# Order of products in the attention pieces, and later slots for three planned steps, in a fused attention and feed-forward kernel

## The chip, the cores and the metric

The kernel runs on one core of a Trainium2 chip. The metric is the device time of one execution in microseconds (us), taken as the median of several runs; less is better. One execution was also recorded by the hardware profiler, and all rows shown come from that record. TensorE is called PE there (its weight loads PEld), VectorE is DVE, ScalarE is ACT, GpSimd is POOL, and SyncE, which issues nearly all DMAs here, is SP.

## What is computed

A decayed linear attention, cut into blocks, feeds a feed-forward network in which two linear maps are multiplied with each other. Batch 4, 8 heads, sequence 768, head size 64; 3072 tokens, model width 512, inner width 1536.

```python
for b in range(nb):                       # blocks of the sequence
    intra = einsum('bhic,bhjc->bhij', qb, kb) * Dmask      # scores, masked
    intra = einsum('bhij,bhjd->bhid', intra, vb)
    inter = einsum('bhid,bhde->bhie', qb * lam_pow, kv_state)
    out[:, :, sl] = intra + inter
    kv_state = lam_block * kv_state + einsum('bhsd,bhse->bhde', kb_dec, vb)
x = out.transpose(0, 2, 1, 3).reshape(B * S, H * D)
return ((x @ w_a) * (x @ w_b)) @ w_out
```

## The kernel before

**Units and groups.** The kernel takes blocks of 128 positions, so a batch has six, and there are 24 units of work (unit u is block u % 6 of batch u // 6; units 5, 11, 17 and 23 are the last blocks of their batches). Units are gathered in groups of 4, 1, 2, 4, 4, 4, 4 and 1 (line 28). The feed-forward part works on one group at a time while the attention of later units is done in between.

**The feed-forward part** (`ffn`, line 518) of a group has slots. In slots 0 to 11, slot f computes inner columns f: four matmuls into an `a_ps` bank, four into a `b_ps` bank (line 468), a copy of the first to SBUF on ScalarE (line 477), and their product `ab` on VectorE (line 495). After them come two slots for each unit of the group, each with half of the output matmuls (`op`, line 515). After each slot `hook` issues the attention steps that `PLAN` (line 43) has for it. Group 2 holds units 5 and 6 and so has slots 0 to 15; group 3 holds units 7 to 10 and has slots 0 to 19.

**The steps in PLAN.** Each engine does its instructions in the order in which they are issued; the schedule is manual, so the order of the program is the order of each queue.
- `P u` prepares a unit. `prep_k` (line 298, alone `PK`) scales k and q on GpSimd (line 276; on VectorE for the k of a few early units), and for units from 7 on issues the DMA transpose of both on SP (line 304). `prep_v` (line 309, alone `PV`) casts v to bf16 on VectorE (line 295; on GpSimd for early units) and calls `pump` (line 188), which issues on SP the loads of q, k and v (line 130) that are next in order, as far ahead as `LOOKAHEAD` and `used["u"]` allow.
- `S u` computes a unit's scores, k by q, into two PSUM banks (`scores`, line 326: 8 matmuls with a 64-row contraction, alternating between the two row halves of the array), and masks them on VectorE (line 349).
- `V u` adds the unit to the running state in PSUM (line 396) and copies it to SBUF on VectorE (`st`, line 429). For the last block of a batch it does nothing.
- `Q (a, b, c, d)` is the pair piece, `pieces_O` (line 442). It takes four banks for the scores of c and d and two for the outputs of a and b, then issues on TensorE: `inter` of a and b (line 380: 8 matmuls a unit, 64 by 64, so that four tiles of the array are in use; none for the first block of a batch; the state of the unit before is read), `scores` of c and d, `intra` of a and b (line 382, masked scores by v), with ScalarE's copies of the outputs to the next groups' x (line 389). Then follow the state products of b for units from 9 on (line 418 or 396), the masks of c and d, and the copy of b's state. `O2` and `O` are the same without c and d.

**Buffers that set order.** PSUM has seven banks in a rotation (`ps_bank`, line 110): `a_ps`, `b_ps`, `op`, scores and outputs all take the next one, and a feed-forward tile skips the bank of the feed-forward tile just before it. `qkT`, the transposed q and k, has five buffers, the loaded q, k and v four each, v in bf16 and scaled q and k six each, the state `st` four. A wait is set for whoever last read a buffer.

Of the kernel before, what the change touches and what calls it, by code (L numbers as in the profile page):

```python
# [22 lines left out]
def _bc(ap, dims):  # L23
# [23 lines left out]
    1: [(0, "V", 4), (2, "T", 5), (3, "PK", 6), (6, "PV", 6), (6, "S", 5), (7, "T", 6),  # L47
        (10, "S", 6), (12, "O2", (5, 6)), (13, "P", 7)],
    2: [(0, "V", 6), (1, "P", 8), (4, "P", 9), (7, "V", 7),
        (9, "S", 7), (9, "S", 8), (6, "P", 10), (10, "V", 8),  # L50
        (12, "Q", (7, 8, 9, 10)), (12, "P", 11), (13, "V", 9), (14, "P", 12),
        (14, "O2", (9, 10))],
    3: [(4, "S", 11), (4, "S", 12)],
}
for _g, _u in ((3, 11), (4, 15), (5, 19)):
    PLAN.setdefault(_g, []).extend(
        [(1, "P", _u + 2), (3, "P", _u + 3), (4, "V", _u),
         (7, "Q", (_u, _u + 1, _u + 2, _u + 3)), (10, "P", _u + 4),
         (12, "P", _u + 5), (13, "V", _u + 2), (16, "Q", (_u + 2, _u + 3, _u + 4, _u + 5))])
PLAN[3] += [(_s, "W", None) for _s in range(12, 19)]  # L60
PLAN[5] = [(_s, _n, (21, 22, 23) if _us == (21, 22, 23, 24) else _us)
# [5 lines left out]
def kernel(  # L67
# [12 lines left out]
    B, H, S, D = q.shape  # L80
# [29 lines left out]
    def ps_bank(name, shape, dt, hold=False, ffn=False, at=None):  # L110
        i = bank["next"] if at is None else at
        while i in bank["held"] or (ffn and i == bank["ffn"]):
            i = (i + 1) % 7
        if ffn:
            bank["ffn"] = i
        bank["next"] = (i + 1) % 7
        if hold:
            bank["held"].add(i)
        return ps_pool.tile(shape, dt, name=name, tag=f"ps{i}")
# [203 lines left out]
    def score_banks():  # L323
        return [ps_bank(f"kq{i}", [128, HP, 128], F32) for i in range(2)]

    def scores(u, kq=None):
        d = U[u]
        kq = kq or score_banks()
        for hp in range(HP):
            for i in range(2):  # L330
                p = slice(64 * i, 64 * i + 64)
                nc.tensor.matmul(kq[i][:, hp, :], lhsT=d["kT"][p, hp, :], rhs=d["qT"][p, hp, :],  # L332
                                 start=True, stop=True, skip_group_check=True)
        return kq

    def masks(u, kq):
        ms = mask(kq)
        U[u]["m"] = lambda i, hp: ms[i][:, hp, :]
# [14 lines left out]
    def o_banks(us, ats=(None, None)):  # L353
        for b, at in enumerate(ats):
            ps = ps_bank("o_ps", [128, 2, 2, BLK], F32, at=at)
            for n, u in enumerate(us):
                U[u].setdefault("o", []).append(ps[:, :, n, :])
        for u in us:
            U[u]["new"] = {(b, half): u == us[0] for b in range(2) for half in range(2)}
            U[u]["flags"] = U[us[0]]["new"]  # L360
# [9 lines left out]
    def inter(u):  # L370
        if u % NB > 0:
            st = st_bufs[(u - 1) % 4]
            for c in range(HP):
                for b in range(2):
                    p = slice(64 * b, 64 * b + 64)
                    o_mm(u, b, c, lhsT=st[p, c, b, :], rhs=U[u]["qT"][p, c, :])

    def intra(u, b):
        for c in range(HP):
            o_mm(u, b, c, lhsT=U[u]["vb"][:, 4 * b + c, :], rhs=U[u]["m"](b, c))  # L380

    def evac_o(us, b, eng="act"):
        xT, col = xTs[us[0]]
        n = len(us)
        o = U[us[0]]["o"][b]
        src = _bc(o, [o.ap[0], [2 * BLK, 2], [1, n * BLK]])
        dst = xT[:, 2 * b:2 * b + 2, col:col + n * BLK]
        if eng == "act":
            nc.scalar.copy(dst, src)  # L389
        else:  # L390
            nc.vector.tensor_copy(dst, src)
# [19 lines left out]
    def kv_beside(u):  # L411
        if u % NB == 0 or u % NB == NB - 1:
            kv_update(u)
            return
        for c in range(HP):
            for b in range(2):
                p = slice(64 * b, 64 * b + 64)
                nc.tensor.matmul(kv["ps"][p, c, b, :], lhsT=U[u]["kn"][:, 2 * c + b, :],
                                 rhs=U[u]["vb"][:, 4 * b + c, :],
                                 start=False, stop=True, skip_group_check=True)  # L420

    def kv_copy(u, ps, eng="dve"):
        st = st_bufs[u % 4]
        if eng == "act":
            for b in range(2):
                p = slice(64 * b, 64 * b + 64)
                nc.scalar.copy(st[p, :, b, :], ps[p, :, b, :])
        else:
            nc.vector.tensor_mul(st[:].rearrange("p c b d -> p c (b d)"),  # L429
                                 ps[:].rearrange("p c b d -> p c (b d)"), bdiag_bc)  # L430
# [11 lines left out]
    def pieces_O(us, nxt=()):  # L442
        kqs = [score_banks() for u in nxt]
        o_banks(us)
        for u in us:
            inter(u)
        for u, kq in zip(nxt, kqs):
            scores(u, kq)
        for b in range(2):
            for u in us:  # L450
                intra(u, b)
            evac_o(us, b)
        beside = len(us) == 2 and us[0] >= n0 + 5
        if beside:
            kv_beside(us[1])
        for u, kq in zip(nxt, kqs):
            masks(u, kq)
        if beside and us[1] % NB < NB - 1:
            kv_copy(us[1], kv["ps"])
# [245 lines left out]
    for g, n in enumerate(GROUPS):  # L705
# [6 lines left out]
        def hook(slot, plan=plan):  # L712
            for name, us in plan.get(slot, ()):
                if name == "C":
                    cast_w("o", us, "dve")
                elif name == "PK":
                    prep_k(us)
                elif name == "PV":
                    prep_v(us)
                elif name == "P":  # L720
                    prep_k(us)
                    prep_v(us)
                elif name == "W":
                    store_kept()
                elif name == "T":
                    piece_T(us)
                elif name == "S":
                    piece_S(us)
                elif name == "V":
                    piece_V(us)  # L730
                elif name == "O":
                    pieces_O((us,))
                elif name == "O2":
                    pieces_O(us)
                else:
                    pieces_O(us[:2], us[2:])
# [31 lines left out]
```

## Time and profile before

| | |
|---|---|
| median of 6 runs | 233.45 us (233.06 to 233.86) |
| profiled execution | 233.54 us |
| its span, first to last instruction | 231.8 us |
| granted TensorE clock, mean | 0.999 |
| TensorE busy | 224.1 us, 97% of the span |
| VectorE, ScalarE, GpSimd busy | 117.3, 89.1, 51.0 us |
| group 2 to the start of group 3 (62 to 82 us) | TensorE busy 19.9 of 20 us |
| group 3 (82 to 116 us) | TensorE busy 32.8 of 34 us |
| groups 4 and most of 5 (116 to 186 us) | TensorE busy 70.0 of 70 us |
| DMA | 39.4 MB in 97541 packets, mean 170 GB/s |

Times in rows are counted from the start of the span. In a timeline row stand start, length, engine, line, operation, output<-inputs, form and count, and in brackets the engine's idle time before it with what ended it; neighbouring like instructions are merged into one row. The ends of matmuls are modelled, and those of a stream overlap, so the starts are what tells the pace. A chain of waits goes back from the last instruction to what released each step. A wait for several semaphores is put down to the one that came last, which need not be the one that was waited for.

### The profile page before, as it was taken

How to read it: one execution, taken by the hardware profiler on the slowest of the kernel's cores; microseconds unless marked ns; L12 is line 12 of the kernel's file. 1: busy time of each engine (PE TensorE's matmuls, PEld its weight loads, DVE VectorE, ACT ScalarE, POOL GpSimd, SP SyncE). 2: the span in 40 equal slices, each digit the busy share in tenths (PEclk: the TensorE clock that was granted, in tenths of full speed). 3: DMA queues.
4: the chain of work that ended last, by engine and by line, in shares of the span. 5: the costliest groups of instructions: out<-in, count | busy, mean ns of one | idle time of the engine just before them, and what ended most of it. 6: DMA issues, size and time to landing. Idle time of an engine off the chain costs nothing.

```text
span 231.8 us, 4653 instructions
## 1 busy us (share of the span) xinstructions
PE 224.1 (97%) x1839; PEld 121.5 (52%) x1839; DVE 117.3 (51%) x205; ACT 89.1 (38%) x172; POOL 51.0 (22%) x65
## 2 busy tenths in 40 slices
PE   7799999999999999899999999999999999999994
PEld 2475444459687644354544454544454544444493
DVE  1894856636579645864335583335583313331050
ACT  3587464067342342232233332334332334432261
POOL 6060000238451356333301534001200000000000
PEclk9999999999999999999999999999999999999999
DMA  4999999999998999999859996239200220000211
GB/s 144 306 264 352 363 387 277 299 201 221 205 208 174 216 188 235 232 195 231 303 193 205 197 216 103 93 101 207 56 3 0 93 90 0 4 0 23 112 48 45
DMA packets 97541, 39.36 MB, mean 170 GB/s; under 512 B 85488, under 2 KB 92016, under 8 KB 97520
## 3 DMA queue, kind: packets, MB, share of 16 engines
q1 hardware_dynamic: 97232, 39.00, 73.6%
q8 instruction: 14, 0.23, 0.4%
q10 hardware_dynamic: 288, 0.07, 0.1%
q14 instruction: 7, 0.06, 0.1%
HBM read 28.32 MB, written 6.29 MB: 149 GB/s over the span
## 4 chain that ended last, share of the span: by engine, by line
PE 78%; DMA 12%; SPq 5%; POOL 2%; DVE 1%; issue 0%; ACT 0%; POOLq 0%
PE op L515 25%; PE b_ps L468 24%; PE a_ps L468 23%; DMA kf<-in_k_dram 4%; SPq L130 3%; DMA wst<-in_moe_w_b_dram 3%; PE o_ps L366 3%; DMA qkT<-qk 2%; DMA q<-in_q_dram 2%; POOL qk L276 2%; PE kq L332 2%; PE kvd L396 1%; SPq L304 1%; SPq L159 1%; PE tps L318 1%
## 5 line engine op out<-in xcount | busy, mean ns | idle before, releaser
L495 DVE TENSOR_TENSOR ab<-a_sb,b_ps 128x512 bf16<-128x512 bf16 (+2 forms) x96 | 52.1, 552 | 73.6 <-PE b_ps L468 54.7
L468 PE MATMUL b_ps<-xT,wb_sb 128*128 128x512 bf16 (+2 forms) x384 | 76.9, 326 | 0.2 <-DVE wb_sb L175 0.2
L468 PE MATMUL a_ps<-xT,wa_sb 128*128 128x512 bf16 (+2 forms) x392 | 76.9, 323 | 0.0
L477 ACT CAST a_sb<-a_ps 128x512 bf16<-128x512 f32 (+2 forms) x96 | 45.2, 481 | 60.8 <-PE a_ps L468 58.8
L515 PE MATMUL op<-wo_sb,ab 128*128 128x512 bf16 (+2 forms) x312 | 65.6, 363 | 0.0
L468 PEld LDWEIGHTS <-wb_sb 128*128 128x128 bf16 x384 | 34.4, 98 | 29.1 <-DVE wb_sb L175 0.7
L468 PEld LDWEIGHTS <-wa_sb 128*128 128x128 bf16 x392 | 34.6, 98 | 27.6 <-DVE wa_sb L175 0.4
L515 PEld LDWEIGHTS <-ab 128*128 128x128 bf16 x312 | 28.7, 98 | 29.9
L349 DVE TENSOR_TENSOR m<-kq,lotri 128x512 bf16<-128x512 f32 x47 | 29.4, 684 | 17.1 <-PE kq L332 17.1
L276 POOL TENSOR_TENSOR qk<-kf,lp_k 128x512 bf16<-128x512 f32 x18 | 18.8, 1043 | 74.0 <-DMA kf<-in_k_dram 57.0
L276 POOL TENSOR_TENSOR qk<-qf,lp_q 128x512 bf16<-128x512 f32 x20 | 23.1, 1153 | 23.4 <-DMA qf<-in_q_dram 23.4
L510 ACT COPY o_sb<-op 128x512 f32<-128x512 f32 (+2 forms) x19 | 10.3, 541 | 34.0 <-PE op L515 34.0
L389 ACT CAST xT<-o_ps 128x512 bf16<-128x512 f32 (+1 forms) x24 | 12.1, 555 | 19.2 <-PE o_ps L366 19.2
L429 DVE TENSOR_TENSOR st<-kvd,bdiag 128x512 bf16<-128x512 f32 x18 | 12.3, 683 | 3.8 <-PE kvd L396 3.8
L295 DVE CAST vb<-vf 128x512 bf16<-128x512 f32 x17 | 10.4, 614 | 4.3 <-DMA vf<-in_v_dram 4.3
L208 PE MATMUL idle<-idle_sb 128*128 128x512 bf16 (+2 forms) x23 | 7.3, 452 | 1.3 <-DVE idle_sb L203 1.3
L366 PE MATMUL o_ps<-m,vb 128*64 128x128 bf16 x192 | 8.0, 222 | 0.0
L332 PE MATMUL kq<-qkT 64*128 64x128 bf16 x160 | 6.8, 218 | 1.2 <-DMA qkT<-qk 1.2
L295 POOL CAST vb<-vf 128x512 bf16<-128x512 f32 x7 | 4.3, 620 | 13.8 <-DMA vf<-in_v_dram 13.8
L169 ACT CAST wb_sb<-wst 128x1024 bf16<-128x1024 f32 x5 | 5.2, 1047 | 5.1 <-DMA wst<-in_moe_w_b_dram 5.1
L320 ACT COPY qkT<-tps 128x1024 bf16<-128x1024 bf16 x3 | 3.0, 1013 | 9.9 <-PE tps L318 9.9
L366 PEld LDWEIGHTS <-vb 128*64 128x64 bf16 x192 | 5.8, 109 | 1.4
(58 smaller groups left out, 81.2 us busy)
## 6 DMA issues: line engine op xcount, KB each, us to landing
vf<-in_v_dram SPq DMA_DIRECT2D x24, 256.0 KB, 4.7
qf<-in_q_dram SPq DMA_DIRECT2D x20, 256.0 KB, 3.9
kf<-in_k_dram SPq DMA_DIRECT2D x20, 256.0 KB, 4.4
out_dram<-o_sb SPq DMA_DIRECT2D x16, 256.0 KB, 2.0
wst<-in_moe_w_a_dram SPq DMA_DIRECT2D x6, 512.0 KB, 9.0
wst<-in_moe_w_b_dram SPq DMA_DIRECT2D x6, 512.0 KB, 9.3
wst<-in_moe_w_out_dram SPq DMA_DIRECT2D x6, 512.0 KB, 10.8
out_dram<-o_kept SPq DMA_DIRECT2D x7, 256.0 KB, 2.5
```

Source lines behind the costliest of these rows:

```text
L276: eng_of(eng).tensor_mul(dst.rearrange("p (c b) d -> p b c d", b=2), x[:].rearrange("p (b c) d -> p b c d", b=2), lp.rearrange("p (b c) o ...
L295: eng_of(eng).tensor_copy(vb, vf)
L332: nc.tensor.matmul(kq[i][:, hp, :], lhsT=d["kT"][p, hp, :], rhs=d["qT"][p, hp, :], start=True, stop=True, skip_group_check=True)
L349: nc.vector.tensor_mul(m, kq[i], lotri_bc)
L366: nc.tensor.matmul(U[u]["o"][b][p, c // 2, :], start=new[b, h % 2], stop=True, skip_group_check=True, **ops)
L389: nc.scalar.copy(dst, src)
L429: nc.vector.tensor_mul(st[:].rearrange("p c b d -> p c (b d)"), ps[:].rearrange("p c b d -> p c (b d)"), bdiag_bc)
L468: nc.tensor.matmul(ps[:, lo:hi], lhsT=w_sb[:, s, f * 128:(f + 1) * 128], rhs=xT[:, s, lo:hi], start=(s == 0), stop=(s == KS - 1), skip_gro ...
L477: nc.scalar.copy(a_sb[:, :gt], ps[:, :gt])
L495: nc.vector.tensor_mul(ab[:, f, :gt], a_sb[:, :gt], ps[:, :gt])
L510: nc.scalar.copy(o_sb[:, lo:hi], op[:, lo:hi])
L515: nc.tensor.matmul(op[:, lo:hi], lhsT=ab[:, f, t * 128:(t + 1) * 128], rhs=wo_sb[:, f, lo:hi], start=(f == 0), stop=(f == FC - 1))
```

## The change

Three edits. In group 2, `P` of unit 10 in slot 6 is split: `PK` stays, and `PV`, the cast of its v with the pump call, goes to slot 11. In group 3, `S` of units 11 and 12 go from slot 4 to slot 6, the `V` of unit 11 from slot 4 to 6, and the pair piece of units 11, 12, 13 and 14 from slot 7 to 9; groups 4 and 5 keep their slots. In `pieces_O` the scores are issued ahead of the inter products instead of behind them, in all seven pair pieces.

```diff
@@ PLAN @@
     2: [(0, "V", 6), (1, "P", 8), (4, "P", 9), (7, "V", 7),
-        (9, "S", 7), (9, "S", 8), (6, "P", 10), (10, "V", 8),
+        (9, "S", 7), (9, "S", 8), (6, "PK", 10), (10, "V", 8), (11, "PV", 10),
         (12, "Q", (7, 8, 9, 10)), (12, "P", 11), (13, "V", 9), (14, "P", 12),
         (14, "O2", (9, 10))],
-    3: [(4, "S", 11), (4, "S", 12)],
+    3: [(6, "S", 11), (6, "S", 12)],
 }
 for _g, _u in ((3, 11), (4, 15), (5, 19)):
     PLAN.setdefault(_g, []).extend(
-        [(1, "P", _u + 2), (3, "P", _u + 3), (4, "V", _u),
-         (7, "Q", (_u, _u + 1, _u + 2, _u + 3)), (10, "P", _u + 4),
+        [(1, "P", _u + 2), (3, "P", _u + 3), (6 if _g == 3 else 4, "V", _u),
+         (9 if _g == 3 else 7, "Q", (_u, _u + 1, _u + 2, _u + 3)), (10, "P", _u + 4),
          (12, "P", _u + 5), (13, "V", _u + 2), (16, "Q", (_u + 2, _u + 3, _u + 4, _u + 5))])
@@ pieces_O @@
         kqs = [score_banks() for u in nxt]
         o_banks(us)
+        for u, kq in zip(nxt, kqs):
+            scores(u, kq)
         for u in us:
             inter(u)
-        for u, kq in zip(nxt, kqs):
-            scores(u, kq)
```

## Prediction

> **What bounds the kernel now.** I read the page first, then TensorE's waits, then the timeline at each place where TensorE stands still, then the chain of waits back from there.
>
> ```profile
> PE 224.1 (97%) x1839; PEld 121.5 (52%) x1839; DVE 117.3 (51%) x205; ACT 89.1 (38%) x172; POOL 51.0 (22%) x65
> ```
>
> TensorE (PE) is busy 97% of 231.8 us, so only its idle time can be won. Its waits over the whole span (us in total, times, longest) have one row that is not start-up:
>
> ```profile
> PE kq L332 <- DMA qkT<-qk: 1.2, 1, 1.2
> ```
>
> The other five rows, 3.1 us together, lie before 22 us. I then went through the starts of single matmuls after 40 us: N=512 follow each other by 0.216 us, N=128 by 0.053 to 0.056 us; every change of array tiling (128x128, 64x64, 64x128, 128x64) adds 0.092 to 0.102 us. Beyond these there are two stalls. The first, in the pair piece of group 3's slot 7:
>
> ```profile
> 96.90 0.31 PE L366 MATMUL o_ps<-qkT,st 64*64 64x128 bf16 x8
> 97.14 0.40 PE L332 MATMUL kq<-qkT 64*128 64x128 bf16 x8
> 98.74 0.40 PE L332 MATMUL kq<-qkT 64*128 64x128 bf16 x8 [1.21 <-DMA qkT<-qk]
> ```
>
> Columns: start, length, what, idle before and who ended it. Unit 13's last scores start at 97.32; unit 14's should follow 0.05 later and come at 98.74: **1.37 us** lost, because the DMA transpose of unit 14 lands at 98.70. The second, in the pair piece of group 2's slot 12, against the same sixteen inter products elsewhere (133.19):
>
> ```profile
> 75.24 0.74 PE L366 MATMUL o_ps<-qkT,st 64*64 64x128 bf16 x16
> ```
> ```profile
> 133.19 0.42 PE L366 MATMUL o_ps<-qkT,st 64*64 64x128 bf16 x16
> ```
>
> 0.74 against 0.42: the first inter product starts at 75.24, the second (b=1, other o_ps bank) at 75.57 instead of 75.29. That bank was f=11's b_ps; VectorE's product that reads it ends at 75.52 (row 75.11 below). **0.28 us** lost. Why unit 14 is late, from the chain of waits:
>
> ```profile
> 81.61 2.24 POOL qk L276 x2
> 83.86 1.75 SPq L304
> 85.66 0.57 SPq L130
> 86.29 4.14 DMA kf<-in_k_dram
> 90.65 2.32 POOL qk L276 x2
> 92.99 5.70 DMA qkT<-qk
> 98.74 0.40 PE kq L332 x8
> ```
>
> A loop of load, two scalings on GpSimd (POOL), transpose, next load. TensorE is not in it, so moving TensorE's work doesn't move it.
>
> **Group 3's pieces, two slots later.** A slot (a_ps and b_ps, 8 x 0.216) is 1.73 us. The pair piece now comes behind f8 and f9: b7's last matmul started at 96.59, b9's would at 96.59 + 3.45 = 100.04, less the 0.28 won earlier = 99.77. Scores start a switch later (100.08), unit 14's 0.23 later: 100.3. The transpose landed at 98.70: slack 1.6 us, stall gone, **-1.37 us**. Scores of 11 and 12 move from slot 4 to 6; their transposes land by 88.06, and they have three slots before their use, as before (4 to 7, now 6 to 9). The step "V" of unit 11 issues nothing: 11 is the last block of its batch. No DMA is issued by these steps, so SP's queue and POOL's keep their order; buffers stay free in time (the transpose of 16, issued at 102.92, overwrites 11's, read last at about 100.7).
>
> What hides the moved work is VectorE's spare time. Slots 6 to 8 hold four masks (2.48) and three products (at 0.60 to 0.69): 4.5 of 5.2 us, the sum of slots 4 to 6 now, after which VectorE idled 0.83. From slot 9's end (T): product 0.9, masks to 3.4, state copy to 4.0, f10's product to 4.7, cast of 15 (0.43 to 0.61) to 5.3, f11's product to 6.1; TensorE needs that one at T + 7.5. v15 landed at 96.18, long before. The first a_ps behind the piece takes the first score bank: in group 4's like piece its mask ends at 134.66 and a_ps starts at 134.79, not delayed. Cost nothing; with that cover gone, each 0.1 us of VectorE lateness beyond some 0.07 costs 0.1.
>
> [...] The rows show that only the first bank is needed at once; I take 0.
>
> **Scores ahead of inter.** Seven pieces. Streaming is the same. Switches before: full to 64x64 0.096, to 64x128 0.095, to 128x64 0.093; after: full to 64x128 0.098, 64x128 to 64x64 (not in the trace), 64x64 to 128x64 0.093. All others lie in 0.092 to 0.102; I take 0.095, so 7 x 0.002 to 0.004 = +0.02 us (ends -0.03 and +0.07). In slot 12 of group 2, scores start at 75.24 (their four banks were emptied by 74.59), inter at 75.79, and the bank is free at 75.57: **-0.28 us**. Elsewhere no inter waits, so nothing is won; masks still queue behind the slot's product.
>
> **Cast of v10, slot 6 to 11.** The rows around it:
>
> ```profile
> 69.24 1.30 POOL L276 TENSOR_TENSOR qk<-qf,lp_q 128x512 bf16<-128x512 f32 x1
> ...
> 78.12 1.04 POOL L276 TENSOR_TENSOR qk<-qf,lp_q 128x512 bf16<-128x512 f32 x1
> ```
> ```profile
> 69.22 0.43 DVE L295 CAST vb<-vf 128x512 bf16<-128x512 f32 x1 [0.20 <-DMA vf<-in_v_dram]
> ...
> 75.11 0.41 DVE L495 TENSOR_TENSOR ab<-a_sb,b_ps 128x256 bf16<-128x256 bf16 x1
> 76.35 2.48 DVE L349 TENSOR_TENSOR m<-kq,lotri 128x512 bf16<-128x512 f32 x4 [0.83 <-PE kq L332]
> 78.75 0.69 DVE L295 CAST vb<-vf 128x512 bf16<-128x512 f32 x1
> 79.37 0.68 DVE L429 TENSOR_TENSOR st<-kvd,bdiag 128x512 bf16<-128x512 f32 x1
> ```
>
> Beside the cast, unit 10's scaling takes 1.30 instead of 1.04. [...] The row says 0.26, and I use it. That scaling heads the loop (transpose of 10, then all loads of 11 and 12), so the loop may run up to 0.26 earlier. In the new place the cast fills 75.5 to 75.9, when POOL is idle (70.5 to 77.1): 0.43. Masks of 9 and 10, which could start at 75.67 now, start at 75.8, still 0.5 before today's 76.35.
>
> Who waits next: in slot 14, inter of unit 10 needs the state copy of 9, which ends at 80.04; that inter started at 80.10, just in time. It is queued behind the cast of v11, which itself is held by unit 11's scaling until 79.16 and not by the masks. TensorE will arrive 0.28 earlier (79.82), the copy is ready 0 to 0.26 earlier (80.10 to 79.84). So of the 0.28, between 0.02 and 0.28 is given back. DMA queues are full there, so I don't count on the whole shift: 0.1.
>
> **Queues.** With the cast its pump call moves, the one that issues the six loads of 11 and 12. On SP nothing lies between the two places, and the loads wait for buffers of 7 and 8 alone; they now start 0.05 after unit 10's transpose: no move.
>
> **Sum**: -1.37 - 0.28 + 0.02 + 0.1 = -1.53. The profiled execution took 233.54 (span 231.8, 1.7 around it): 232.0. The median, 233.45, is 0.09 below it: **231.9 us**.
>
> **Rivals.**
> (A) As summed: 231.9, and 231.4 to 232.2 with the runs' spread and the loop's full shift or half of it; 0.68.
> (B) The wait goes to the state copy in full (the loop doesn't shift, and TensorE stands 0.28 in slot 14), which gives 232.1; with one mask's 0.6 less the margin of 0.07 lost behind slot 9 as well, 232.6; to 232.8 with a slow draw. For it: 80.04 against 80.10 is no margin. 0.18.
> (C) The change doesn't do what it says: stalls return whole behind slot 9, for example in the first a_ps and in f10's bank. It needs VectorE 1.4 us late where the sum has 0.07 to 1.3 us in hand: 233.3; 0.07.
> (D) Slower: the loads of 11 and 12 do follow the cast to slot 11. They would start at 75.9 instead of 71.86, v11 lands at 82.1 instead of 78.10, its cast blocks VectorE, and the state copy of 9 comes at 82.1 + 0.43 + 0.68 = 83.2; slot 14 waits 3.4 us from 79.8. Net -1.65 + 3.4: 235.2. It decides from a slip of 1.6 us on, since each us of slip is one of TensorE. Against it: SP's order of waits. 0.04. Another 0.03 for other losses.
>
> This kernel's six runs spread 233.06 to 233.86, so about 0.2% (0.47 us) can be told. Faster takes A, B and a little of C: 0.88; within 0.2%: 0.06; slower: 0.06. The range reaches from A with the loop's full gain and a fast draw, 231.3, to B's end, 232.8.
>
> **What would show it.** TensorE's waits have no row for kq; kq in slot 9 is gapless at about 100.1; the first inter of slot 12 shows no hole and starts near 75.8; POOL's scaling at 69.2 takes 1.04; the first load of 11 starts at 71.6 to 71.9; the last chain leaves out kf and qkT. Wrong if a_ps behind slot 9 shows a gap, or o_ps at 79.7 waits over 0.3, or the loads start near 76.

## The result and the profile after

The changed kernel takes 232.10 us (median of 15 runs, 231.59 to 233.07), the kernel before 233.27 us in the same measurement (34 runs, 232.30 to 235.42). The ratio is 0.9949 with a 95% interval of 0.9932 to 0.9967: 1.19 us less, between 0.77 and 1.59. The forecast of the sum was 1.53 less. Ratios, here and below, leave out the few executions that took over 1.5% more than the fastest of their kernel, and they are not the quotient of the two medians. The profiled executions differ by 1.58 (233.54 and 231.96; spans 231.8 and 230.2).

The busy line of the page after, and TensorE's waits over the whole span after:

```profile
PE 223.2 (97%) x1839; PEld 121.0 (53%) x1839; DVE 117.5 (51%) x205; ACT 88.9 (39%) x172; POOL 50.0 (22%) x65
```
```profile
PE tq L597 <- DVE scratch L587: 1.4, 3, 0.8
PE idle L208 <- DVE idle_sb L203: 1.3, 1, 1.3
PE tk L597 <- DVE scratch L587: 0.4, 2, 0.2
PE b_ps L468 <- DVE wb_sb L175: 0.2, 1, 0.2
PE tn L617 <- ACT scratch L608: 0.2, 1, 0.2
```

The row kq <- DMA qkT is gone, and what is left lies in the start-up. Busy time hardly moved, for the gain is idle time. TensorE's timeline after, at the pair piece of group 3 (now behind slot 9) and at that of group 2's slot 12:

```profile
100.15 0.62 PE L332 MATMUL kq<-qkT 64*128 64x128 bf16 x16
100.70 0.31 PE L366 MATMUL o_ps<-qkT,st 64*64 64x128 bf16 x8
```
```profile
75.40 0.62 PE L332 MATMUL kq<-qkT 64*128 64x128 bf16 x16
75.95 0.42 PE L366 MATMUL o_ps<-qkT,st 64*64 64x128 bf16 x16
```

Line 366 is that of a helper, which both `inter` (from line 370, form 64*64) and `intra` (from line 378, form 128*64) use. All sixteen scores of units 13 and 14 run without a hole, and the sixteen inter products take 0.42 again instead of 0.74. Starts of the same instructions in both profiles say where the time came from:

| first matmul of | before | after | difference |
|---|---|---|---|
| the output part of group 0 | 39.22 | 39.42 | +0.20 (start-up, code the same) |
| the pair piece of slot 12, group 2 | 75.24 | 75.40 | +0.16 |
| inter of units 9 and 10, slot 14 | 79.95 | 79.78 | -0.17 |
| the pair piece of slot 16, group 3 | 113.57 | 111.99 | -1.58 |
| the pair piece of slot 7, group 4 | 133.19 | 131.61 | -1.58 |

Slot 12 gave 0.33 us, group 3 gave 1.41, and nothing more was gained after that.

VectorE and GpSimd after, at the places that the prediction named:

```profile
75.64 0.42 DVE L295 CAST vb<-vf 128x512 bf16<-128x512 f32 x1
75.97 2.48 DVE L349 TENSOR_TENSOR m<-kq,lotri 128x512 bf16<-128x512 f32 x4
78.37 0.42 DVE L295 CAST vb<-vf 128x512 bf16<-128x512 f32 x1
78.70 0.69 DVE L429 TENSOR_TENSOR st<-kvd,bdiag 128x512 bf16<-128x512 f32 x1
```
```profile
68.71 1.04 POOL L276 TENSOR_TENSOR qk<-qf,lp_q 128x512 bf16<-128x512 f32 x1
76.13 1.04 POOL L276 TENSOR_TENSOR qk<-kf,lp_k 128x512 bf16<-128x512 f32 x1 [6.38 <-PE kq L332]
77.13 1.04 POOL L276 TENSOR_TENSOR qk<-qf,lp_q 128x512 bf16<-128x512 f32 x1
```

The cast of v10 takes its 0.42 while GpSimd is idle; the scaling of unit 10's q takes 1.04 instead of 1.30. The cast of v11 comes after GpSimd's last scaling has ended (78.17), is not held up (0.42 us, before 0.69), and the state copy ends at 79.38, ahead of the inter products at 79.78.

### The profile page after: what moved, and what is told of

The parts are those of the page before. It is cut to its first block, busy times and chain, and to the rows that moved or that the text cites. A ratio compares the mean times of both kernels' runs of the same rounds, so it can differ in the third digit from the quotient of the medians.

```text
span 230.2 us, 4653 instructions
## 1 busy us (share of the span) xinstructions
PE 223.2 (97%) x1839; PEld 121.0 (53%) x1839; DVE 117.5 (51%) x205; ACT 88.9 (39%) x172; POOL 50.0 (22%) x65
## 4 chain that ended last, share of the span: by engine, by line
PE 89%; DMA 5%; SPq 3%; DVE 0%; issue 0%; ACT 0%
PE op L515 27%; PE b_ps L468 27%; PE a_ps L468 26%; PE o_ps L366 4%; DMA wst<-in_moe_w_b_dram 3%; PE kq L332 2%; SPq L130 2%; DMA q<-in_q_dram 2%; PE kvd L396 1%; SPq L159 1%; PE tps L318 1%; DVE wb_sb L175 0%; PE kvd L418 0%; SPq L224 0%; ACT o_sb L510 0%
## 5 line engine op out<-in xcount | busy, mean ns | idle before, releaser
L276 POOL TENSOR_TENSOR qk<-qf,lp_q 128x512 bf16<-128x512 f32 x20 | 22.0, 1102 | 22.7 <-DMA qf<-in_q_dram 22.7
L208 PE MATMUL idle<-idle_sb 128*128 128x512 bf16 (+2 forms) x23 | 6.3, 400 | 1.3 <-DVE idle_sb L203 1.3
L332 PEld LDWEIGHTS <-qkT 64*128 64x128 bf16 x160 | 4.5, 94 | 4.2 <-issue 3.2
```

The costliest lines, as they stand in the source:

```text
L276: eng_of(eng).tensor_mul(dst.rearrange("p (c b) d -> p b c d", b=2), x[:].rearrange("p (b c) d -> p b c d", b=2), lp.rearrange("p (b c) o ...
```

## The experiments

Two theories at first. The stall theory: TensorE lost 1.4 us to unit 14's transpose and 0.3 to a bank, the slots remove the one and the order the other. The loop theory: the cast's move makes loads and transposes earlier, and that is the gain. A third was that the order itself is worth something in each piece. Differences in us below are worked out from the ratio and its 95% interval; kernels of one batch ran on one chip beside the kernel before (233.85, 233.69 and 234.37 us in the three batches).

**slots_only.** Of the change, only this:

```diff
-    3: [(4, "S", 11), (4, "S", 12)],
+    3: [(6, "S", 11), (6, "S", 12)],
...
-        [..., (4, "V", _u), (7, "Q", ...), ...]
+        [..., (6 if _g == 3 else 4, "V", _u), (9 if _g == 3 else 7, "Q", ...), ...]
```

> Only group 3's steps stand two slots later; order and cast as before. Stall theory (the wait for unit 14's transpose is the main cost, and it is paid by position alone): the row kq <- DMA qkT disappears, the hole of 0.28 us in group 2's slot 12 stays; 1.0 to 1.4 us faster than before, nearly all that the whole change gave (1.2 by medians). Loop theory (the cast's move made the loads and transposes earlier, and the slots matter little): under 0.4 us faster. Order theory: under 0.3 us faster.

Measured 232.66; ratio 0.9939 (0.9912 to 0.9966), 1.43 us less (0.80 to 2.06). TensorE's waits have no row for kq. The slots alone carry the gain. Its profile also shows what unit 10's cast can do in slot 6. VectorE, then TensorE:

```profile
70.98 0.43 DVE L295 CAST vb<-vf 128x512 bf16<-128x512 f32 x1 [1.40 <-DMA vf<-in_v_dram]
```
```profile
72.72 0.60 PE L468 MATMUL a_ps<-xT,wa_sb 128*128 128x256 bf16 x4 [0.27 <-DVE ab L495]
...
76.70 0.41 PE L366 MATMUL o_ps<-qkT,st 64*64 64x128 bf16 x15 [0.39 <-DVE ab L495]
```

v10 landed at 70.89 in this execution and not at 69.13. The cast held VectorE for it, the products behind it came late, and TensorE lost 0.34 and 0.57 us (by the starts). Some 0.3 of the 0.57 is slot 12's own hole, which this kernel keeps. In slot 11 the cast comes some 5 us later (75.64 in the profile after, against 70.98), when v10 has long landed.

**order_only.** Only the swap in `pieces_O`:

```diff
+        for u, kq in zip(nxt, kqs):
+            scores(u, kq)
         for u in us:
             inter(u)
-        for u, kq in zip(nxt, kqs):
-            scores(u, kq)
```

> Only the scores stand ahead of the inter products; slots and cast as before. Stall theory: 0.28 us is won in group 2's slot 12, but unit 14's transpose lands by its own clock, so that gain goes into a longer wait in slot 7; and the 0.24 us of inter work that stood ahead of the wait now stands behind it. Net 0.0 to 0.25 us slower than before. Order theory (the order itself is the gain): 0.5 us or more faster. Loop theory: no change.

Measured 234.06; ratio 1.0002 (0.9978 to 1.0025). No gain, though the hole in slot 12 is gone. TensorE in slot 7 of this kernel:

```profile
96.68 0.40 PE L332 MATMUL kq<-qkT 64*128 64x128 bf16 x8
98.64 0.40 PE L332 MATMUL kq<-qkT 64*128 64x128 bf16 x8 [1.56 <-DMA qkT<-qk]
98.96 0.31 PE L366 MATMUL o_ps<-qkT,st 64*64 64x128 bf16 x8
```

TensorE arrives earlier and waits longer: 1.72 us by the starts instead of 1.37, until the same moment (98.64 and 98.74). The inter products that used to stand ahead of the wait now follow it. What is won ahead of a wait that another engine's work ends is lost in that wait. The order theory (0.5 us or more) falls: the interval only just reaches 0.5.

**cast_only.** Only unit 10's cast and pump call:

```diff
-        (9, "S", 7), (9, "S", 8), (6, "P", 10), (10, "V", 8),
+        (9, "S", 7), (9, "S", 8), (6, "PK", 10), (10, "V", 8), (11, "PV", 10),
```

> Only unit 10's cast and pump call stand in slot 11; order and slots as before. Stall theory: GpSimd's scaling of unit 10's q takes 1.04 instead of 1.30 us, the loop is some 0.26 earlier and the wait for unit 14 that much shorter: 0 to 0.3 us faster. Loop theory: 0.8 us or more faster, the wait for unit 14 gone. The pump theory (loads of 11 and 12 follow the cast to slot 11): first load of 11 near 76 instead of 71.9 us, 1 us or more slower.

Measured 233.53; ratio 0.9982 (0.9950 to 1.0014): -0.42 us, not told from nothing. The wait for unit 14 is still there, 0.92 us by the starts:

```profile
98.26 0.40 PE L332 MATMUL kq<-qkT 64*128 64x128 bf16 x8 [0.76 <-DMA qkT<-qk]
```

The time alone would leave room for the loop theory's 0.8; the wait that it has gone is still there, so it falls. So does the theory of the pump: the first load of 11 starts at 70.84 and not near 76.

**no_cast.** Slots and order, the cast left in slot 6 (the line of cast_only undone).

> Order and slots as changed, unit 10's cast left in slot 6. Stall theory: both stalls gone; in slot 14 of group 2 the inter products of unit 10 wait up to 0.28 us for the state copy if the scaling is at 1.30 us and the loop not earlier; within 0.3 us of the whole change. Loop theory: about as slow as before.

Measured 232.20; ratio 0.9922 (0.9889 to 0.9954), 1.82 us less (1.08 to 2.60). In its profile both stalls are gone and no other shows. The cast's move isn't needed for the gain.

**slots_cast.** Slots and cast, the order as before (the swap undone), in the third batch.

> The changed kernel with the inter products ahead of the scores again (slots and cast as changed). Stall theory: the hole of 0.28 to 0.33 us in group 2's slot 12 is back and nothing else, so 0.0 to 0.3 us slower than the changed kernel (part of it would have been given back in slot 14 anyway). Order theory: 0.5 us or more slower.

Measured 232.44; ratio 0.9935 (0.9915 to 0.9955). The only hole behind 26 us is slot 12's, 0.32 by the starts:

```profile
75.40 0.79 PE L366 MATMUL o_ps<-qkT,st 64*64 64x128 bf16 x16
76.12 0.62 PE L332 MATMUL kq<-qkT 64*128 64x128 bf16 x16
```

The changed kernel took 232.27 beside it, 0.17 less: as expected, and too small to be told from its runs.

**after_again.** The changed kernel once more, in the same batch.

> The changed kernel once more, beside the others on this chip: 0.3 to 0.7% below before. A second profile shows whether TensorE's waits behind 26 us are absent in every execution or, as in slot8 and dve_late, come and go in slot 14 of group 2 (state copy of unit 9 behind the cast of v11).

Measured 232.27; ratio 0.9927 (0.9906 to 0.9948). In this execution inter of unit 10 in slot 14 waited 0.11 us:

```profile
79.81 0.56 PE L366 MATMUL o_ps<-qkT,st 64*64 64x128 bf16 x16
```

0.56 instead of 0.42. So that wait comes and goes.

**whole_p11.** The changed kernel with all of unit 10's preparation in slot 11:

```diff
-        (9, "S", 7), (9, "S", 8), (6, "PK", 10), (10, "V", 8), (11, "PV", 10),
+        (9, "S", 7), (9, "S", 8), (10, "V", 8), (11, "P", 10),
```

> The changed kernel with all of unit 10's preparation (both scalings, transpose, cast, pump call) in slot 11. Queue theory (a slot sets the order within each queue and nothing else; between the two places neither GpSimd nor SP has another instruction): order of both queues the same, scaling of unit 10 near 68 to 69 us, first load of 11 near 71, time of the changed kernel within 0.3 us. Slot theory (work starts when TensorE comes to its slot): the scaling comes after 74 us, loads and transposes of the units behind some 5 us later, over 1 us slower than the changed kernel.

Measured 232.27; ratio 0.9948 (0.9924 to 0.9972), as the changed kernel. GpSimd and SP:

```profile
67.97 1.04 POOL L276 TENSOR_TENSOR qk<-kf,lp_k 128x512 bf16<-128x512 f32 x1 [2.44 <-PE b_ps L468]
68.97 1.04 POOL L276 TENSOR_TENSOR qk<-qf,lp_q 128x512 bf16<-128x512 f32 x1
```
```profile
71.33 0.57 SPq L130 DMA_DIRECT2D qf<-in_q_dram  x1
```

Issued behind TensorE's slot 11 in the program, the scaling still runs at 68 us, some six slots ahead of it. It starts 0.16 us after the k of unit 10 has landed (67.81). The bracket names TensorE, but the lag is the same as in the profile before (68.08 and 68.24), where the wait is put down to the DMA. Between these two places, where neither queue has another instruction, the slot set the order within each queue and nothing else.

**slot8.** Group 3's steps one slot later than before instead of two:

```diff
-    3: [(6, "S", 11), (6, "S", 12)],
+    3: [(5, "S", 11), (5, "S", 12)],
...
-         (9 if _g == 3 else 7, "Q", ...
+         (8 if _g == 3 else 7, "Q", ...
```

> The changed kernel with group 3's steps one slot later than before instead of two: scores of 11 and 12 in slot 5, the pair piece in slot 8, where TensorE reaches unit 14's scores near 98.6. If unit 14 lands with all shares in time (96.7 to 97.2): no wait, the time of the changed kernel. If its sixteenth share is late (98.2 to 98.7): a wait of 0 to 0.2 us. Either way within 0.3 us of the changed kernel: the second slot is only margin.

Measured 232.85; ratio 0.9988 (0.9961 to 1.0016). A miss by the medians: 0.58 us above whole_p11, which ran beside it (the two intervals overlap). In its profile the loop was late (unit 10's transpose issued at 72.03, after at 69.78), unit 14 landed at 100.25 and scores waited 0.27. More was lost in slot 14. VectorE and TensorE there:

```profile
79.70 0.91 DVE L295 CAST vb<-vf 128x512 bf16<-128x512 f32 x1 [0.77 <-DMA vf<-in_v_dram]
80.53 0.68 DVE L429 TENSOR_TENSOR st<-kvd,bdiag 128x512 bf16<-128x512 f32 x1
```
```profile
80.31 0.31 PE L366 MATMUL o_ps<-qkT,st 64*64 64x128 bf16 x8
81.26 0.31 PE L366 MATMUL o_ps<-qkT,st 64*64 64x128 bf16 x8 [0.64 <-DVE st L429]
```

That is rival B's mechanism, at 0.81 us by the starts: v11 landed late (79.61, after 77.17), its cast held the state copy, the inter products of unit 10 waited. This is in group 2, ahead of every step that slot8 moves, so slot 8 isn't its cause, and how much of the 0.58 is the slot's can't be said. The second slot is margin that some executions use.

**v11_later.** An attempt to take that wait out: the cast of v11 goes behind both state copies, its pump call stays in place.

```diff
-        (12, "Q", (7, 8, 9, 10)), (12, "P", 11), (13, "V", 9), (14, "P", 12),
+        (12, "Q", (7, 8, 9, 10)), (12, "PK", 11), (13, "V", 9), (14, "P", 12), (15, "PV", 11),
...
                 elif name == "PK":
-                    prep_k(us)
+                    prep_k(us); pump()
```

> The changed kernel with the cast of unit 11's v moved from slot 12 to slot 15 of group 2, behind the state copies of 9 and 10; its pump call stays in slot 12, so SP's order is unchanged. If the late state copy is what the changed kernel still loses in some executions (0.26 and 0.8 us in two profiles), the median falls by 0.0 to 0.4 us against the changed kernel and no profile has a wait in slot 14. If the spread comes from the start-up alone: no difference.

Measured 232.35; ratio 0.9928 (0.9908 to 0.9949), against 232.27 for the changed kernel beside it. Slot 14 has no wait, and the time is the same. Its profile lost 1.28 us in the start-up instead (a_ps behind wa_sb at 20.6 us, by the starts), in code that is the same. No version here is told from the changed kernel as faster.

**dve_late.** The changed kernel with two casts more on VectorE, ahead of the masks of group 3's pair piece; nothing reads them.

```diff
                 else:
+                    [nc.vector.tensor_copy(late_b, late_f) for _ in range(2 * (us[0] == 11))]
                     pieces_O(us[:2], us[2:])
```

> The changed kernel with two more casts of 128x512 on VectorE (of a zero tile that nothing reads) ahead of the masks of group 3's pair piece in slot 9, so that the masks come some 0.67 us later. Cover theory (the first a_ps behind the piece waits for the first score bank and has some 0.07 us in hand): a hole of about 0.6 us in front of that a_ps, waiting for VectorE's mask, and 0.6 us more than the changed kernel. If VectorE's work is truly hidden there: no hole, no difference.

Measured 233.43; ratio 0.9998 (0.9968 to 1.0029), 1.16 above whole_p11 beside it. VectorE, then TensorE:

```profile
101.63 0.88 DVE L736 CAST late_b<-late_f 128x512 bf16<-128x512 f32 x2
102.43 2.47 DVE L349 TENSOR_TENSOR m<-kq,lotri 128x512 bf16<-128x512 f32 x4
```
```profile
102.21 0.40 PE L396 MATMUL kvd<-vb,qk 128*128 128x128 bf16 x4
103.17 1.02 PE L468 MATMUL a_ps<-xT,wa_sb 128*128 128x512 bf16 x4 [0.56 <-DVE m L349]
```

The casts start where the masks would have, and the masks 0.80 us later; the a_ps behind the piece starts 0.72 us late. The cover is 0.08 us, as thin as the prediction put it (0.07), and VectorE's lateness beyond it is paid one for one. In group 2 this execution also lost 0.16 us in the scores of slot 9 and 0.26 in slot 14.

**before_again.** The kernel before, profiled again.

> The kernel before, profiled a second time. Fetch theory: whether the sixteenth share of unit 14's transpose is late differs from execution to execution, so the wait in slot 7 lies between 0 and 1.7 us. If it is fixed by the program: 1.4 us again.

One time, 233.67. TensorE in slot 7:

```profile
97.75 0.40 PE L332 MATMUL kq<-qkT 64*128 64x128 bf16 x8
98.84 0.40 PE L332 MATMUL kq<-qkT 64*128 64x128 bf16 x8 [0.70 <-DMA qkT<-qk]
```

0.86 us by the starts, not 1.37: unit 14 landed at nearly the same time (98.80 and 98.70), but TensorE came later, since its start-up was 0.65 longer. The size of the wait belongs to the execution.

**fetch_shift.** Why unit 14 lands late was followed further. A DMA here completes in sixteen parts, and the trace has the time of each. For unit 14's transpose (us):

```
                15th part  16th part   TensorE code block of 16 KiB
before            97.17      98.70       96.45 to 97.41
before_again      97.30      98.80       96.56 to 97.51
order_only        96.97      98.59       96.29 to 97.25
cast_only         96.70      98.21       95.97 to 96.93
whole_p11         97.07      98.60       96.38 to 97.37
after_again       97.40      98.86       96.67 to 97.65
v11_later         98.07      99.61       97.34 to 98.29
after             96.73      96.74       96.01 to 96.99
no_cast           96.63      96.68       95.93 to 96.92
```

In seven of fourteen profiles, among them all four with slot 7 and an unchanged start, the last part is 1.5 us late. In the kernel before, fifteen parts were there at 97.17, ahead of TensorE's need at 97.37: the whole wait is that one part. In the other three with slot 7 and the old start the fifteenth part came 0.6 us and more ahead of TensorE's need or, in order_only, 0.06 behind it: without the late part there is next to no stall. And in whole_p11, after_again and v11_later the part was late too (98.60, 98.86, 99.61), but TensorE came to unit 14's scores at 100.38, 100.55 and 100.88 and did not wait. So it is the later slot that removes the stall, and not an early landing.

Close to the late part the record of DMA packets has a 16 KiB block on queue 8 (0.95 to 0.99 us long) and an 8 KiB block on queue 14; the page calls what both queues move "instruction", here called code. That queue 8 is TensorE's is read from this test, in which its block moves from 96.45 to 89.39 us. The test moves TensorE's code blocks, by 78 more entries in its stream at the start:

```diff
-    warm(13, 512)
+    warm(52, 128)
```

> The kernel before, with its 13 warming matmuls of 512 columns at the start made 52 of 128 columns: the same columns in all, 78 more entries in TensorE's instruction stream, all ahead of the first real product. The code blocks of 16 KiB that are fetched for TensorE then come some 8 us earlier (near 88 instead of 96 us). Fetch theory (one of the sixteen shares of unit 14's transpose is held up by code fetches on the same DMA engine, 1.5 us in each kernel that kept slot 7): the sixteenth completion comes with the other fifteen at about 97.2, the wait in slot 7 is under 0.4 us instead of 1.4, and the time is 0.7 to 1.4 us less than before, near the changed kernel. Loop theory (the loop alone sets when unit 14 lands): the wait stays at 1.0 to 1.7 us and the time does not change.

Measured 235.30; ratio 1.0060 (1.0029 to 1.0092), 1.40 us more. The expectation on the time failed. On the place it held in part: the block came at 89.39, the sixteenth part of unit 14 came with the others (98.41, though issued at 93.55, 0.56 later than before), and the wait was 0.49 by the starts. The profiled execution was the quickest of its twelve (233.26), so its trace doesn't show what cost most of the others over 1 us; the edit changes the start-up itself as well as the place of the blocks. The cause of the late part isn't settled: in after and no_cast the block lies just as near and no part is late.

## Why the prediction was right

**Slots.** Right in the place of the stall and in what removes it. Scores of 13 and 14 start at 100.15 (100.08 forecast) without a wait, and slots_only gives the gain by itself. Only half right is why unit 14 was late: the prediction put all of it down to the loop, but fifteen of the sixteen parts that the loop brought were there in time, and the last came 1.53 us behind them (fetch_shift). So 1.37 us was a mis-sized term: it was one execution's wait, taken for all. Four profiles with slot 7 and the old start have 1.37, 0.86, 0.92 and 1.72. The view of qkT in the trace of before, between 80 and 100 us, had the warning, for the 5.7 is unit 14's transpose:

```profile
DMA to landing us min/median/max: 4.0/4.2/5.7
```

With 1.05, the mean of the three waits with the old order, the prediction's sum would be 1.21 less instead of 1.53 (an estimate made afterwards). The measured 1.19 goes that way, but its interval reaches to 1.59, so the time doesn't tell the two apart. That the time itself came within 0.2 us (232.10 against 231.9) is in part luck: the kernel before took 233.27 in this measurement, 0.18 less than in the runs that the forecast started from.

**Order.** The 64x128 to 64x64 switch, not in the trace before, took 0.093 (0.095 taken), and the switch from full to 64x64 is 0.093 and not 0.096 in the starts of before. The three switches sum to 0.28 us in both orders, so the order costs nothing. No piece of the profile after waits for a mask, though dve_late shows that 0.08 us is all that stands between. The bank's 0.28 was 0.33 in slot 12 by the starts; in the time it isn't told from the spread (slots_cast).

**Cast.** The scaling fell from 1.30 to 1.04. The sum used it only in part, and rightly: no_cast has 1.04 there too with the cast in slot 6, and in slots_only that cast, at 70.98, comes behind the scaling (69.70, 1.04 us), so it depends on whether the two happen to meet. The loop did run 0.79 us earlier after (unit 10's transpose was issued at 69.78 instead of 70.57), but not for the cast: order_only, which leaves it in slot 6, has 69.72, and after_again, which moves it, 70.84. What the step may be worth, and the prediction didn't see, is in slots_only: with the cast in slot 11 a late v10 doesn't hold VectorE in slot 6. Neither cast_only (-0.42, interval across zero) nor no_cast gives it a size.

**The wait in slot 14.** 0.1 was put down as given back. It was 0 in after and 0.11 in after_again; 0.26 and 0.81 in dve_late and slot8, whose loop was late. So the wait of rival B is real in some executions, and in one of them larger than its 0.28; the time that B gave (232.1 and more) can't be told from A's, and v11_later, which takes the wait out, is no faster.

**Rivals.** C did not happen: no wait behind slot 9. D did not either: the first load of 11 starts at 71.07 in after and 71.33 in whole_p11, not 76; the forecast of 71.6 to 71.9 was missed to the early side, with the loop.

## What to carry to other kernels

Before a stall is put into a sum at its full length, ask how far the waited-for DMA stood from its own usual latency: one execution's wait is a draw (0.86 to 1.72 us in four profiles), and the margin that removes it should be larger than the spread (with one slot of margin, slot8 still waited 0.27 us). A gain ahead of a wait that another engine's work ends is worth nothing until that wait is gone (order_only: 0.0). An instruction that waits for a DMA on an in-order engine belongs as late in that queue as its user allows, since all that stands behind it waits too (slots_only shows such a wait, 1.40 us of VectorE's time, with 0.34 and 0.57 us lost on TensorE; no run here gives the move a size).

## What was not expected of the hardware

One of a DMA's sixteen parts was late by 1.5 us in seven of fourteen profiles while the other fifteen came within some 0.3 us (96.89 to 97.17 in the kernel before). In the profile before, queue 8 moved 14 blocks of code of 16 KiB, the other code queue 7 of 8 KiB:

```profile
q8 instruction: 14, 0.23, 0.4%
...
q14 instruction: 7, 0.06, 0.1%
```

Of TensorE's holes behind 26 us in the profiles before and after none is left over for code. Whether the blocks hold up other transfers stays open here. And 78 entries more in TensorE's stream, with the same number of columns, cost 1.40 us (0.68 to 2.15): whether by where the code blocks fall or by what those matmuls do to the start-up was not found out.
